# Merging the first transfers of two weights, and halving four sums on GpSimd, in an attention and bilinear-FFN kernel

## The chip, the cores and the metric

The kernel runs on one core of a Trainium2 chip. The metric is the device time of one execution in microseconds (us). A profile is one traced execution; its span is some 1.7 us shorter than the time of the same run (245.2 against 246.89). PE is TensorE, PEld its weight load, DVE is VectorE, ACT is ScalarE, POOL is GpSimd.

A run is labelled slow when it is over 1.5% above the fastest run of the same kernel in the same set. The label compares a kernel only with itself: where all runs of a kernel are equally long, all are labelled fast.

## The reference, cut to what matters

```python
a  = softmax(phi over the sequence)                     # 8 batches, 8 heads, 576 tokens, 32 memories
k_m, v_m = a^T k, a^T v                                 # per head: 32 x 64
x  = softmax(q k_m^T / 8) v_m                           # 4608 tokens x 512
out = ((x @ w_a) * (x @ w_b)) @ w_out                   # 512 -> 1536 -> 512
```

The kernel never forms `x`. It folds `v_m` into the two up weights `w_a` and `w_b` once per batch ("fold"), and multiplies the folded weights (`vab`) by the normalised attention `A`. For the down weight it uses a scheme with fewer products, which needs four sums of quarters of `w_out`; GpSimd makes these once.

## The kernel before

The parts that the argument touches, with cuts marked by `...`:

```python
def load_wab(lo, hi):                     # a column block of both up weights
    nc.gpsimd.dma_start(out=wa_sb[:, :, lo:hi], in_=wa_rows[:, :, lo:hi])
    nc.gpsimd.dma_start(out=wb_sb[:, :, lo:hi], in_=wb_rows[:, :, lo:hi])
...
load_wab(0, 256)
...
load_wab(256, 512)
load_wab(512, 1024)
load_wab(1024, 1536)
load_wo(0)                                # then phi, k, q, v of batch 1, and load_wo(1), load_wo(2)
...
def normalise(g, ...):                    # A = E * R, both in SBUF
    ...
    engine = nc.vector if b < 3 else nc.gpsimd
    engine.tensor_tensor(out=attn[b][:, g, sl], in0=t["E"][:, g, sl], in1=t["R", g][:, sl], op=ALU.mult)
...
def sum_weights():                        # four sums of quarters of the down weight
    t = [w_sums[:, x] for x in range(4)]
    for out, in0, in1 in ((t[0], quarter(0, 1), quarter(0, 0)), (t[1], quarter(1, 1), t[0]),
                          (t[2], quarter(1, 1), quarter(0, 1)), (t[3], quarter(1, 0), t[1])):
        nc.gpsimd.tensor_tensor(out=out, in0=in0, in1=in1, op=ALU.subtract)
...
fill(16)                                  # idle matmuls that wake TensorE's clock
chain(0, "... nr10 nr11 hv0a hx0a")
ups(steps(0, 0, 4), slots(0, "hv0b+hx0b hv1a+hx1a - hv1b+hx1b - v1a+x1a - v1b+x1b"))
load(2)
ups(steps(0, 4, 12), slots(0, "- - - - v2a+x2a+v2b+x2b - -"))
chain(1, "exp0 exp1 y9 ks0 ... vt0 y1 vt1 nr1 hv0a hx0a hv0b y3 hx0b y2")
load(3)                                   # phi, k, v, q of batch 3, issued by GpSimd
sum_weights()                             # and directly behind q's issue, the sums
```

The strings are a plan: `v0a` is the fold of 512 columns (block 0) of `w_a`, `x0a` moves it from PSUM into `vab`; `hv0a` and `hx0a` do so for 256 columns; `nr1` is `normalise` for the second half of the heads; `f2` is two idle matmuls; `y9` nine matmuls of earlier output. In the profiles `pva` is the output of a fold, and `pa` and `pb` are the two up products of one tile of tokens (a "group" is one of them, four matmuls).

The softmax here doesn't subtract the row's maximum and nothing guards it: scores larger than these inputs give would overflow.

Of the kernel before, what the change touches and what calls it, by code (L numbers as in the profile page):

```python
# [11 lines left out]
ALU = mybir.AluOpType  # L12
# [6 lines left out]
def kernel(  # L19
# [11 lines left out]
    nc = tc.nc  # L31
# [60 lines left out]
    def load(b):  # L92
        load_phi(b)
        load_k(b)
        load_v(b)
        load_q(b)

    def load_wab(lo, hi):
        nc.gpsimd.dma_start(out=wa_sb[:, :, lo:hi], in_=wa_rows[:, :, lo:hi])
        nc.gpsimd.dma_start(out=wb_sb[:, :, lo:hi], in_=wb_rows[:, :, lo:hi])  # L100
# [46 lines left out]
    def fill(n, cols=512):  # L147

        pw = banks.tile([P, 512], F32, name="pw")
        for _ in range(n):  # L150
            nc.tensor.matmul(pw[:, :cols], warm[:, :P], warm[:, :cols], start=True, stop=True)
# [2 lines left out]
    make_identity(nc, ident)  # L154
    nc.vector.memset(kv_sbs[0][:, 2], 1.0 / CS)
    nc.vector.tensor_copy(out=kvs[0][:, 0, 0:2], in_=k_f32)
    load_wab(0, 256)

    ones = consts.tile([P, 4, 32], F16, name="ones")
    nc.vector.memset(ones, 1.0)  # L160
# [1 line left out]
                            pattern=[[-32, 4], [0, 32]], channel_multiplier=1)  # L162
    nc.gpsimd.affine_select(out=ones, in_=ones, compare_op=ALU.is_ge, fill=0.0, base=31,
                            pattern=[[32, 4], [0, 32]], channel_multiplier=-1)
    load_wab(256, 512)
    load_wab(512, 1024)
    load_wab(1024, 1536)
    load_wo(0)
# [249 lines left out]
    KH = NFF // 2  # L418
# [3 lines left out]
    def quarter(x, y):  # L422
        return wo_sb[:, KH * x:KH * (x + 1), NH * y:NH * (y + 1)]

    def sum_weights():
        t = [w_sums[:, x] for x in range(4)]
        for out, in0, in1 in ((t[0], quarter(0, 1), quarter(0, 0)), (t[1], quarter(1, 1), t[0]),
                              (t[2], quarter(1, 1), quarter(0, 1)), (t[3], quarter(1, 0), t[1])):
            nc.gpsimd.tensor_tensor(out=out, in0=in0, in1=in1, op=ALU.subtract)

    def tokens_of(cidx, x):
        pair, c = divmod(cidx, NI)
# [151 lines left out]
    def up(b, i, hfs):  # L584
        A, vab = attn[b], vabs[b]
        base = S * (b % 2)
        fs = slice(P * i, P * (i + 1))
        a_sbs = []
        for hf in hfs:
            pa = banks.tile([P, HALF], F32, name="pa")  # L590
            for g in range(2):
                nc.tensor.matmul(pa, vab[0][:, g, fs], A[:, g, HALF * hf:HALF * (hf + 1)],  # L592
                                 start=(g == 0), stop=(g == 1))
            a_sb = apool.tile([P, HALF], F16, name="a_sb")
            nc.scalar.copy(out=a_sb, in_=pa)  # L595
            a_sbs.append(a_sb)
        if len(hfs) > 1:
            yield
        for hf in hfs:
            pb = banks.tile([P, HALF], F32, name="pb")  # L600
            for g in range(2):
                nc.tensor.matmul(pb, vab[1][:, g, fs], A[:, g, HALF * hf:HALF * (hf + 1)],  # L602
                                 start=(g == 0), stop=(g == 1))
            t0 = base + HALF * hf
            nc.vector.tensor_tensor(out=ht[:, i, t0:t0 + HALF], in0=a_sbs[hf - hfs[0]], in1=pb, op=ALU.mult)  # L605
        yield

    def ups(steps, side=()):

        side = iter(side)  # L610
        for step in steps:
            for _ in up(*step):
                work.advance()
                next(side, us[step[0]]["-"])()
        for f in side:
            work.advance()
            f()

    def steps(b, lo, hi):

        return [(b, i, (0, 1)) for i in range(lo, hi)]
# [14 lines left out]
    def slots(b, names):  # L636

        def both(fs):
            return lambda: [f() for f in fs]
        def unit(n):  # L640
            if n == "fin":
                return lambda: work.pull(-work.done % NFF)
            if n == "L":
                return lambda: load(b + 2) if b + 2 < B else None
            if n[0] == "y":
                return lambda: some(int(n[1:]))
            if n[0] == "d" and n[1:].isdigit():
                return lambda: work.pull(int(n[1:]))
            return us[b + n.endswith("'") - n.endswith("_")][n.rstrip("'_")]

        return [both([unit(n) for n in x.split("+")]) for x in names.split()]
# [3 lines left out]
    def some(n):  # L655
        for _ in range(n):
            next(early, None)

    def chain(b, plan):


        for x in plan.split():
            if x[0] == "f":
                fill(int(x[1:]), 256)
            elif x[0] == "y":
                some(int(x[1:]))
            else:
                us[b][x]()

    fill(16)  # L670
    chain(0, "exp0 exp1 ks0 kt0 qt0 qt1 f2 s0 e0 ks1 kt1 den0 qt2 qt3 f2 s1 nr0 e1 vs0 vs1 den1 vt0 vt1 nr10 nr11 hv0a hx0a")
    ups(steps(0, 0, 4), slots(0, "hv0b+hx0b hv1a+hx1a - hv1b+hx1b - v1a+x1a - v1b+x1b"))
    load(2)
    ups(steps(0, 4, 12), slots(0, "- - - - v2a+x2a+v2b+x2b - -"))
    chain(1, "exp0 exp1 y9 ks0 y3 kt0 qt0 qt1 y1 y3 ks1 qt2 s0 e0 y6 kt1 qt3 den0 y3 s1 nr0 e1 y4 y2 den1 vs0 vs1 vt0 y1 vt1 nr1 hv0a hx0a hv0b y3 hx0b y2")
    load(3)
    sum_weights()
    ups(steps(1, 0, 4), slots(1, "- hv1a+hx1a hv1b+hx1b+y1 - v1a+x1a y3+v1b x1b y3"))
    ups(half_steps(1, 0, 4), slots(1, "- v2a+x2a+v2b+x2b+qt0' - - qt1'+exp0'+qt2' exp1' - kv'+km'+y9"))
# [43 lines left out]
```

## Time and profile before

The median is 247.02 us (246.88 to 247.04, 3 runs).

| | before |
|---|---|
| span of the profiled run | 245.2 us |
| TensorE busy | 232.1 us, 95% |
| VectorE, ScalarE, GpSimd busy | 69%, 65%, 63% |
| last weight block used by TensorE | 30.31 us, after a wait of 1.15 us |
| GpSimd's four sums of the down weight | 49.31 to 61.71 us |

TensorE is the bound of the whole, but until 30.3 us the transfers are; the prediction shows the lines.

```profile
48.09 0.45 DVE L325 TENSOR_TENSOR A<-E,R 128x576 f16<-128x576 f16 x1
```

Look at the 0.40 us in which GpSimd idles between the issue of v and the issue of q. VectorE starts its product `A`, two inputs from SBUF, at 48.09, 0.06 us before the issue of v ends (47.41 + 0.74 = 48.15), and does most of it in this gap. Nothing in the program orders the product and the issue of q. Below, the issue of v is called v3 and that of q is called q3, as they are for batch 3.

### The profile page before, as it was taken

What the parts mean: (1) busy time and instruction counts of PE and PEld (TensorE: products, weight loads), DVE (VectorE), ACT (ScalarE), POOL (GpSimd) and SP (SyncE); (2) the same over time, 40 slices, a digit from 0 to 9 for tenths busy, and PEclk for the clock granted to TensorE, in tenths of its full rate; (3) what the DMA queues carried; (4) which work ended last, traced back from release to release, by engine and by line L of the source; (5) the groups of instructions that cost most, each with busy time, mean ns of one, the idle gap of its engine ahead of it and who ended that gap; (6) DMA issues with size and microseconds to landing.
All of it is one profiled execution on the core that took longest, in us unless ns stands there. A gap on an engine that the chain in (4) does not pass through costs nothing.

```text
span 245.2 us, 7629 instructions
## 1 busy us (share of the span) xinstructions
PE 232.1 (95%) x3016; PEld 165.1 (67%) x3016; DVE 168.9 (69%) x406; ACT 158.2 (65%) x409; POOL 154.0 (63%) x126
## 2 busy tenths in 40 slices
PE   7689799999998999999999999999999999999993
PEld 3334474456665857777787777877787877888882
DVE  3455783468959958876995549866996576756742
ACT  2364672678697489578856858577856867565330
POOL 8733263499799028892899769892849177937001
PEclk9977999999999999999999999999999999999999
DMA  6999999999979803973059832598130303032254
GB/s 202 208 198 207 206 257 207 256 218 283 225 190 207 166 1 104 239 133 88 20 138 220 189 86 44 148 189 184 23 68 3 86 3 87 4 87 53 45 128 118
DMA packets 26099, 33.81 MB, mean 138 GB/s; under 512 B 1968, under 2 KB 20528, under 8 KB 26064
## 3 DMA queue, kind: packets, MB, share of 16 engines
q0 software_dynamic: 19344, 22.84, 51.0%
q1 hardware_dynamic: 6208, 9.70, 16.0%
q10 hardware_dynamic: 512, 0.79, 1.0%
q8 instruction: 23, 0.38, 0.6%
q14 instruction: 12, 0.10, 0.1%
HBM read 42.47 MB, written 9.44 MB: 212 GB/s over the span
## 4 chain that ended last, share of the span: by engine, by line
PE 82%; DMA 11%; DVE 3%; issue 1%; ACT 1%; POOL 1%; DVEq 0%; POOLq 0%
PE pa L592 19%; PE pb L602 18%; PE py L462 17%; PE pv L462 8%; DMA wb_sb<-in_moe_w_b_dram 7%; PE pva L337 5%; PE po L389 5%; DMA kv_sb<-in_v_dram 4%; PE px L462 4%; PE pkv L213 2%; PE pD L314 2%; PE pscore L292 1%; PE pT L242 1%; PE pk L256 1%; POOL q_sb L90 1%
## 5 line engine op out<-in xcount | busy, mean ns | idle before, releaser
L605 DVE TENSOR_TENSOR ht<-a_sb,pb 128x288 f16<-128x288 f16 x192 | 83.0, 449 | 41.8 <-ACT a_sb L595 29.2
L595 ACT CAST a_sb<-pa 128x288 f16<-128x288 f32 x192 | 74.9, 406 | 31.0 <-PE pa L592 29.0
L592 PE MATMUL pa<-A,vab 128*128 128x288 f16 x384 | 76.8, 288 | 1.5 <-DVE A L325 1.1
L602 PE MATMUL pb<-A,vab 128*128 128x288 f16 x384 | 77.3, 289 | 0.8 <-ACT vab L349 0.6
L444 POOL TENSOR_TENSOR h_sums<-ht 128x768 f16<-128x768 f16 x28 | 45.9, 1641 | 38.7 <-DVE ht L605 37.3
L602 PEld LDWEIGHTS <-vab 128*128 128x128 f16 x384 | 37.4, 99 | 13.7 <-issue 1.7
L592 PEld LDWEIGHTS <-vab 128*128 128x128 f16 x384 | 34.6, 98 | 15.7 <-issue 8.5
L462 PEld LDWEIGHTS <-h_sums 128*128 128x128 f16 x384 | 37.4, 98 | 6.9 <-issue 0.4
L349 ACT CAST vab<-pva 128x512 f16<-128x512 f32 (+1 forms) x52 | 28.1, 559 | 13.1 <-PE pva L337 13.1
L349 DVE CAST vab<-pva 128x512 f16<-128x512 f32 (+1 forms) x52 | 32.7, 644 | 3.1 <-PE pva L337 2.5
L462 PEld LDWEIGHTS <-ht 128*128 128x128 f16 x288 | 28.2, 98 | 5.6 <-issue 0.4
L462 PE MATMUL py<-w_sums,h_sums 128*128 128x256 f16 x192 | 30.3, 272 | 0.0
L444 POOL TENSOR_TENSOR h_sums<-h_sums,ht 128x768 f16<-128x768 f16 x14 | 23.1, 1648 | 1.0
L444 POOL TENSOR_TENSOR h_sums<-ht,h_sums 128x768 f16<-128x768 f16 x14 | 23.0, 1642 | 1.0
L305 ACT ACTIVATE E<-pscore 128x288 f16<-128x288 f32 x32 | 11.4, 416 | 11.3 <-PE pscore L292 11.2
L325 POOL TENSOR_TENSOR A<-E,R 128x576 f16<-128x576 f16 x10 | 12.8, 1276 | 7.0 <-ACT R L323 6.8
L462 PE MATMUL py<-wo_sb,ht 128*128 128x256 f16 x96 | 16.0, 273 | 0.0
L462 PE MATMUL pv<-w_sums,h_sums 128*128 128x256 f16 x96 | 16.0, 272 | 0.0
L469 ACT ACTIVATE u<-py 128x256 f32<-128x256 f32 x32 | 12.4, 388 | 5.2 <-PE py L462 4.9
L462 PE MATMUL py<-w_sums,ht 128*128 128x256 f16 x96 | 15.5, 272 | 0.1
L462 PE MATMUL px<-wo_sb,ht 128*128 128x256 f16 x96 | 15.4, 273 | 0.0
L204 DVE STREAM_TRANSPOSE qT<-q_sb 128x288 f32<-128x288 f32 x32 | 14.3, 462 | 0.6 <-DMA q_sb<-in_q_dram 0.6
(64 smaller groups left out, 262.9 us busy)
## 6 DMA issues: line engine op xcount, KB each, us to landing
out_dram<-o_sb SPq DMA_DIRECT2D x68, 128.0 KB, 2.5
kv_sb<-in_v_dram POOLq DMA_DIRECT2D x7, 576.0 KB, 11.1
phi_sb<-in_phi_dram POOLq DMA_DIRECT2D x7, 576.0 KB, 4.8
kv_sb<-in_k_dram POOLq DMA_DIRECT2D x7, 576.0 KB, 8.6
q_sb<-in_q_dram POOLq DMA_DIRECT2D x6, 576.0 KB, 14.0
wo_sb<-in_moe_w_out_dram POOLq DMA_DIRECT2D x3, 512.0 KB, 16.3
q_sb<-in_q_dram POOLq DMA_DIRECT2D x4, 288.0 KB, 12.5
wa_sb<-in_moe_w_a_dram POOLq DMA_DIRECT2D x2, 512.0 KB, 14.9
```

The source lines that it names most:

```text
L204: nc.vector.transpose(out=t["qT"][:, hp, :].bitcast(F32), in_=qs[b][:, hp, :].bitcast(F32))
L325: engine.tensor_tensor(out=attn[b][:, g, sl], in0=t["E"][:, g, sl], in1=t["R", g][:, sl], op=ALU.mult)
L337: nc.tensor.matmul(t["pva", lo, z][g][0][32 * j:32 * j + 32, 0:hi - lo], t["kvT"][64 * r:64 * r + 64, 4 + g, M * j:M * j + M], w_sbs[z][64 ...
L349: engine_copy(out=vabs[b][z][:, g, lo:hi], in_=pva[:, 0:hi - lo])
L389: nc.tensor.matmul(po, ht[:, i, P * c:P * (c + 1)], wo_sb[:, i, :], start=(i == 0), stop=(i == NFF - 1))
L444: engine.tensor_tensor(out=out, in0=in0, in1=in1, op=op)
L462: nc.tensor.matmul(po, lhs[:, i], rhs[:, i], start=first and i == 0, stop=i == KH - 1, skip_group_check=not first)
L469: nc.scalar.mul(out=x, in_=po, mul=scale)
L592: nc.tensor.matmul(pa, vab[0][:, g, fs], A[:, g, HALF * hf:HALF * (hf + 1)], start=(g == 0), stop=(g == 1))
L595: nc.scalar.copy(out=a_sb, in_=pa)
L602: nc.tensor.matmul(pb, vab[1][:, g, fs], A[:, g, HALF * hf:HALF * (hf + 1)], start=(g == 0), stop=(g == 1))
L605: nc.vector.tensor_tensor(out=ht[:, i, t0:t0 + HALF], in0=a_sbs[hf - hfs[0]], in1=pb, op=ALU.mult)
```

## The change

Its intent: fewer, larger transfers for the first block of the up weights, the folds of which then come in one piece; and shorter GpSimd instructions, so that VectorE is held off for less time by each.

```diff
-    load_wab(0, 256)
+    load_wab(0, 512)
...
-    load_wab(256, 512)
     load_wab(512, 1024)
...
-            nc.gpsimd.tensor_tensor(out=out, in0=in0, in1=in1, op=ALU.subtract)
+            for x in range(2):
+                sl = slice(KH // 2 * x, KH // 2 * (x + 1))
+                nc.gpsimd.tensor_tensor(out=out[:, sl], in0=in0[:, sl], in1=in1[:, sl], op=ALU.subtract)
...
-    chain(0, "... nr10 nr11 hv0a hx0a")
-    ups(steps(0, 0, 4), slots(0, "hv0b+hx0b hv1a+hx1a - hv1b+hx1b - v1a+x1a - v1b+x1b"))
+    chain(0, "... nr10 nr11 v0a x0a")
+    ups(steps(0, 0, 4), slots(0, "v0b+x0b - - - - v1a+x1a - v1b+x1b"))
```

More of the change, by code (lines that the diff above doesn't have):

```diff
@@ L670 @@
     fill(16)
-    chain(0, "exp0 exp1 ks0 kt0 qt0 qt1 f2 s0 e0 ks1 kt1 den0 qt2 qt3 f2 s1 nr0 e1 vs0 vs1 den1 vt0 vt1 nr10 nr11 hv0a hx0a")
-    ups(steps(0, 0, 4), slots(0, "hv0b+hx0b hv1a+hx1a - hv1b+hx1b - v1a+x1a - v1b+x1b"))
+    chain(0, "exp0 exp1 ks0 kt0 qt0 qt1 f2 s0 e0 ks1 kt1 den0 qt2 qt3 f2 s1 nr0 e1 vs0 vs1 den1 vt0 vt1 nr10 nr11 v0a x0a")
+    ups(steps(0, 0, 4), slots(0, "v0b+x0b - - - - v1a+x1a - v1b+x1b"))
     load(2)
```

## The prediction

> **What bounds the kernel now.** I read the page first, then the chain that ended last in order of time for the first 40 us, then GpSimd's and TensorE's timelines of that stretch, then tables by stretch cut at the steps of the granted clock. The page gives the frame:
>
> ```profile
> PE 232.1 (95%) x3016; PEld 165.1 (67%) x3016; DVE 168.9 (69%) x406; ACT 158.2 (65%) x409; POOL 154.0 (63%) x126
> ```
>
> TensorE is the bound of the whole, but not of its beginning. The chain in order of time says:
>
> ```profile
> 3.60 10.12 DMA kv_sb<-in_v_dram
> ...
> 14.01 16.26 DMA wb_sb<-in_moe_w_b_dram
> ...
> 30.31 0.41 PE pva L337 x8
> 30.72 0.60 PE pb L602 x4
> ```
>
> Until 30.3 us the end is set by transfers: the last one is the third block (columns 1024 to 1536) of the second up weight. After that the chain is nearly all matmuls. So a change before 30.3 us moves the end only if it moves that landing, or makes TensorE so late that it no longer waits for it. How much room there is stands in TensorE's timeline:
>
> ```profile
> 16.39 0.69 PE L337 MATMUL pva<-wa_sb,kvT 64*32 64x256 f16 x8
> 17.56 0.66 PE L592 MATMUL pa<-A,vab 128*128 128x288 f16 x4 [0.48 <-ACT vab L349]
> 18.16 0.30 PE L337 MATMUL pva<-wb_sb,kvT 64*32 64x256 f16 x8
> 19.05 1.14 PE L602 MATMUL pb<-A,vab 128*128 128x288 f16 x4 [0.59 <-ACT vab L349]
> ...
> 28.75 0.41 PE L337 MATMUL pva<-wa_sb,kvT 64*32 64x512 f16 x8
> 30.31 0.41 PE L337 MATMUL pva<-wb_sb,kvT 64*32 64x512 f16 x8 [1.15 <-DMA wb_sb<-in_moe_w_b_dram]
> ```
>
> The slack is 1.15 us: TensorE could arrive that much later at 30.31 for nothing. GpSimd's timeline shows when weights land, because its 13th issue waits for the 5th to land, the 14th for the 6th and so on (eight in flight):
>
> ```profile
> 16.53 0.74 POOL L104 DMA_DIRECT2D wo_sb<-in_moe_w_out_dram  x1 [1.79 <-DMA wa_sb<-in_moe_w_a_dram]
> 17.71 0.75 POOL L78 DMA_DIRECT2D phi_sb<-in_phi_dram  x1 [0.44 <-DMA wb_sb<-in_moe_w_b_dram]
> 19.03 0.74 POOL L82 DMA_DIRECT2D kv_sb<-in_k_dram  x1 [0.56 <-DMA wa_sb<-in_moe_w_a_dram]
> 20.36 0.70 POOL L90 DMA_DIRECT2D q_sb<-in_q_dram  x1 [0.59 <-DMA wb_sb<-in_moe_w_b_dram]
> ```
>
> The four 256 KB pieces landed just before 16.5, 17.7, 19.0 and 20.4 us. The 512 KB pieces after them came 2.5 to 2.6 us apart (issues at 22.93, 25.50, 28.02, 30.55). Last, the table by stretch (columns: stretch, length, busy of PE, PEld, DVE, ACT, POOL, granted clock, DMA share, GB/s):
>
> ```profile
> 12.08:15.50 3.42, 3.42 (x105) 1.74 (x102) 2.06 (x6) 2.37 (x6) 0.74 (x1) 0.50 1.38 199
> 15.50:18.91 3.41, 1.83 (x28) 0.65 (x24) 1.66 (x6) 2.38 (x8) 1.49 (x2) 1.00 1.42 198
> 18.91:22.32 3.41, 3.27 (x20) 1.60 (x20) 1.44 (x5) 1.25 (x4) 1.44 (x2) 0.50 1.25 207
> 22.32:25.73 3.41, 3.41 (x43) 1.68 (x42) 2.91 (x8) 2.21 (x6) 0.98 (x2) 1.00 1.24 206
> 32.56:245.20 212.64, 206.09 (x2662) 152.15 (x2660) 150.70 (x363) 142.33 (x371) 137.94 (x98) 1.00 0.62 127
> ```
>
> The transfers never pause: about 200 GB/s in every stretch, and 198 against 206 while the small pieces move. The clock falls to half in stretches of 3.41 us that follow a sparse one (1.83 us busy at 15.50 to 18.91). From 32.56 us on TensorE is 97% busy (206.09 / 212.64) at the full clock.
>
> **What the Trainium skill says.** "TensorE: Matmul & The Clock Gate", section "Part 1: The HAM clock gate", has windows of about 3.4 us, half rate after an idle window and full rate after a busy one. The trace agrees in length and in direction; where the limit lies it leaves open (2.27 us busy kept the clock, 2.24 lost it). "DMA: Bandwidth & Descriptors", section "Rules for kernel authors", advises coalescing transfers, and under "Why small descriptors are slow (HBM only)" gives a fixed cost per packet; here it shows only as the 198 against 206 GB/s. "GPSIMD Engine Reference", section "1. Specifications", says that its SBUF interface is shared with VectorE, with contention when a VectorE instruction has two SBUF inputs. The trace agrees elsewhere: a product of A at 73.28 us, both inputs in SBUF, took 1.46 us beside a GpSimd sum, against 0.46 without.
>
> **Part one, the transfers.** Four pieces of 256 KB become two of 512 KB, in the order a, b instead of a, b, a, b. Bytes and queue order behind them stay.
> - Columns 0 to 512 of a land where two pieces did, at about 17.4 us instead of 16.3; those of b where four did, at about 20.0 instead of 17.5.
> - What comes behind them gains the lower packet cost: 1 MB at 206 instead of 198 GB/s, 5.1 instead of 5.3 us, so 0.2 us. The last block lands at about 30.05 instead of 30.27. Two issues fewer let GpSimd queue the next ones earlier, which is worth nothing as the queue is never empty.
>
> **Part two, the folds of the first batch.** Removed: two 256-column folds and their evictions; the remaining two become 512 wide (0.41 instead of 0.30 us at full clock; evictions 0.59 and 0.69 instead of 0.37 and 0.42). Step by step:
> - fold of a at 17.4, evicted by 18.5; pa of tile 0 at 18.6 instead of 17.56.
> - fold of b at 20.0; twice 0.41 if at half clock, then 0.69 of eviction: pb of tile 0 at 21.4 instead of 19.05, 2.35 us late.
> - then no fold stands between pa1, pb1, pa2 and pb2. In the kernel before there are two, 0.41 and 0.30, and their waits.
> At full clock four matmuls of a group take 0.49 us (chain: 0.49 for pa and pb), at half about 0.95 (20.47 to 21.40 in the timeline). The fold of block 1 of a, at 23.94 before, comes after five groups:
> - (i) clock full from 22.32: 21.4 + 0.95 + 4 x 0.49 = 24.3 us. The rest follows as before about 0.35 late, well inside the 1.15 us. TensorE then waits for the last block, and the end moves by -0.2.
> - (ii) clock half until 25.73: by then four and a half groups are done; the fold is at about 26.0, 2.05 late. From there seven groups and two folds remain before block 2: 7 x 0.49 + 2 x 0.41 = 4.25, so 30.25, and with block 2's two folds, 0.82 (0.41 each), pb of tile 6 at 31.05 against 30.65: +0.4. ScalarE and VectorE must evict without a gap in this catch-up, so I count up to +0.7.
> Which one comes is set by the window 18.91 to 22.32. In it TensorE now waits for b's transfer for over a microsecond, so it is busy about 2.2 us instead of 3.27, which is at the undecided limit. I give (ii) 6 in 10.
>
> **Part three, the halves.** Four sums of 3.09 us (49.31 to 61.71) become eight of 128x768, a shape that GpSimd does in 1.64 us in the token sums, starts 1.65 us apart (63.14, 64.86, 66.57, 68.17, 69.75): 8 x 1.65 = 13.2 instead of 12.4, so an end at 62.5. The next GpSimd work starts at 63.14 after an idle 1.43 us, so 0.6 us of room remain. VectorE in this stretch does only products from PSUM, casts from PSUM and transposes, at their usual 446, 688 and 455 ns, so nothing waits for a GpSimd sum that a shorter one would free: 0 us.
>
> **Sum.** 0.4 x (-0.2) + 0.6 x (+0.4) is +0.15 us; the end of (ii) leans upward. 247.02 + 0.1 = 247.1 us.
>
> **Rivals.**
> - The up weights become the bound earlier and TensorE never catches up: late by the full 2.35 us at pb0 less the 1.15 us of slack, +1.2, 248.2 us. For it: the half clock. Against it: two folds fewer and 0.49 us groups with all weights there.
> - The merge is hidden altogether and only the packet cost counts: 246.8 us. For it: the 1.15 us wait at 30.31. It is my case (i).
> - The merge makes all later transfers a good deal earlier: between the landing of v (13.72) and of the first piece (16.3) lie 2.6 us where 1.3 would do, and if the small packets cause that, the last block is 1.3 us earlier, 245.9 us. Against it: the rate in that time is 198 GB/s, so bytes were moving and only their order is odd.
> - The halves let VectorE in between and speed up the stretch from 49 to 62 us: at most some tenths, as VectorE's durations there are normal.
>
> **Range and chances.** Low end: (i) with some of the early landing, 246.4. High end: (ii) with a clumsy catch-up, 248.0. Two per cent are 4.9 us; all rivals lie within 1.3. Faster 0.01, same 0.975, slower 0.015.
>
> **What would show it.** The granted clock in 22.3 to 25.7 us tells (i) from (ii). The fold of a near 17.4 us, pb of tile 0 near 21.4. The wait at the last block's fold: about 1 us in (i), none in (ii). Eight sums of about 1.64 us, ending near 62.5, with an idle gap after them. It would be wrong if the last block landed over 0.5 us off 30.05, if the lead or lag at 32 us did not reach the end, or if the token sums started later than 63.1 by more than TensorE's own lag.

## More of the kernel before

Timeline columns: start, length, engine, line, operation, tiles, count, and in brackets the idle time before it and what ended that.

```profile
47.41 0.74 POOL L85 DMA_DIRECT2D kv_sb<-in_v_dram  x1 [2.24 <-PE pT L274]
48.55 0.74 POOL L90 DMA_DIRECT2D q_sb<-in_q_dram  x1 [0.40 <-DVE A L325]
49.31 3.11 POOL L429 TENSOR_TENSOR w_sums<-wo_sb 128x1536 f16<-128x1536 f16 x1
```

## The result, and the profile after

Four runs of the changed kernel took 246.72, 261.45, 247.32 and 262.68 us. Two are labelled fast and two slow. Four runs of the kernel before, in the same rounds, took 246.88 to 247.10. The ratio of fast runs is 1.0001, with an interval of 0.9976 to 1.0025. Here and below a ratio is the mean time of one kernel's fast runs over that of the other's of the same rounds, so it is not quite the ratio of the medians that are quoted. The median of all four runs, 254.38, is a time that no run had.

The profiled run was a fast one, with a span of 245.0 us. On its page, TensorE's row of busy times is:

```profile
PE 231.8 (95%) x3000; PEld 165.3 (67%) x3000; DVE 168.4 (69%) x404; ACT 157.9 (64%) x407; POOL 153.0 (62%) x128
```

There are 16 matmuls fewer, the two folds of eight that fell away, and two more instructions on GpSimd: two issues fewer, four sums more. TensorE's timeline in the first 31 us:

```profile
17.30 0.63 PE L336 MATMUL pva<-wa_sb,kvT 64*32 64x512 f16 x8 [0.85 <-DMA wa_sb<-in_moe_w_a_dram]
18.62 1.14 PE L593 MATMUL pa<-A,vab 128*128 128x288 f16 x4 [0.70 <-ACT vab L348]
19.77 0.63 PE L336 MATMUL pva<-wb_sb,kvT 64*32 64x512 f16 x8
21.10 1.14 PE L603 MATMUL pb<-A,vab 128*128 128x288 f16 x4 [0.70 <-ACT vab L348]
...
29.86 0.41 PE L336 MATMUL pva<-wa_sb,kvT 64*32 64x512 f16 x8
30.09 0.40 PE L336 MATMUL pva<-wb_sb,kvT 64*32 64x512 f16 x8
30.42 0.66 PE L603 MATMUL pb<-A,vab 128*128 128x288 f16 x4
```

The beginning is 2.05 us later than before (pb of tile 0 at 21.10 against 19.05), but the last fold has no bracket any more: the wait of 1.15 us for the last block is gone, and TensorE leaves this part 0.23 us earlier (30.42 against 30.65). The chain that ended last has only one piece of transfer in this stretch, the first, and matmuls and evictions (moves from PSUM to SBUF) from there on:

```profile
4.92 12.24 DMA wa_sb<-in_moe_w_a_dram
17.30 0.70 PE pva L336 x6
```

GpSimd's timeline shows the last landing by the issue that waits for it, 0.36 us earlier than before (30.55):

```profile
30.19 0.70 POOL L85 DMA_DIRECT2D kv_sb<-in_v_dram  x1 [1.87 <-DMA wb_sb<-in_moe_w_b_dram]
```

The table by stretch (columns as in the prediction) shows the granted clock in the stretches that the prediction was undecided about:

```profile
18.91:22.32 3.41, 2.70 (x18) 1.27 (x17) 1.13 (x2) 1.38 (x3) 0.70 (x1) 0.50 1.24 208
22.32:25.73 3.41, 3.41 (x27) 2.13 (x26) 2.12 (x7) 1.71 (x5) 1.41 (x2) 0.76 1.24 205
```

The clock came back within the second stretch, 0.76 on average: between the prediction's two cases. The trace's clock records have it at half from 17.15 to 23.98 us, two windows of 3.41 us, which do not lie where the stretches, cut by the steps of the kernel before, do. So far everything is small and near the prediction. It does not explain the two runs of 261 and 263 us. The first profile shows nothing of them, since it was a fast run.

### The profile page after: what moved, and what is told of

Its sections match the earlier page's. It is cut to its first block, busy times and chain, and to the rows that moved or that the text cites. A ratio compares the mean times of both kernels' runs of the same rounds, so it can differ in the third digit from the quotient of the medians.

```text
span 245.0 us, 7595 instructions
## 1 busy us (share of the span) xinstructions
PE 231.8 (95%) x3000; PEld 165.3 (67%) x3000; DVE 168.4 (69%) x404; ACT 157.9 (64%) x407; POOL 153.0 (62%) x128
## 4 chain that ended last, share of the span: by engine, by line
PE 86%; DMA 5%; DVE 3%; ACT 2%; POOL 1%; issue 1%; DVEq 0%; POOLq 0%
PE pa L593 21%; PE pb L603 20%; PE py L463 17%; PE pv L463 8%; PE pva L336 6%; DMA wa_sb<-in_moe_w_a_dram 5%; PE po L388 5%; PE px L463 4%; PE pkv L212 2%; PE pD L313 2%; PE pscore L291 1%; PE pT L241 1%; ACT vab L348 1%; PE pk L255 1%; POOL q_sb L90 1%
## 5 line engine op out<-in xcount | busy, mean ns | idle before, releaser
L470 ACT ACTIVATE u<-py 128x256 f32<-128x256 f32 x32 | 12.4, 388 | 5.2 <-PE py L463 4.9
```

Source lines behind the costliest of these rows:

```text
L470: nc.scalar.mul(out=x, in_=po, mul=scale)
```

## The experiments

The theory at the outset: the long runs are of the kernel's own making, something in the stretch of GpSimd's sums that happens or not by a small difference in timing. The rival: they are a slower state of the chip, which any kernel may meet, and the clock of 0.95 in them is its cause. A second question was which of the two parts of the change is at fault. All kernels gave correct results. Kernels of one set ran on the same chip beside the kernel before.

### First set (kernel before: 247.03 to 247.47 us, 11 runs)

**The changed kernel again** (no edit), for a trace of a long run.

> The changed kernel once more, with more runs, because two of its first four came out at 261.5 and 262.7 us at a mean granted clock of 0.954 and 0.957, against 246.7 and 247.3 us at 0.986 and 0.972; the kernel before had four runs within 0.2 us. Theory S (the slow runs are the change's own: its sparser beginning meets the clock windows at an unlucky moment): about half of the runs are slow again, the kernel before beside it on the same chip has none. Rival C (a state of the chip or of its neighbours that hits any kernel): no slow run, or as many in the kernel before. The fast runs by both: 246.5 to 247.4 us, ratio 0.998 to 1.002.

Measured: 261.97, 262.39, 262.83 and 261.72 us; ratio 1.0606 (1.0593 to 1.0620). All are long here, so they are labelled fast. The kernel before ran at 247.0 to 247.5 between them on the same chip, so a slower state of the chip falls as the cause. The trace has the cause in one line of VectorE's timeline:

```profile
48.92 13.90 DVE L324 TENSOR_TENSOR A<-E,R 128x576 f16<-128x576 f16 x1
```

The product that took 0.45 us took 13.90. GpSimd's timeline beside it:

```profile
48.25 0.74 POOL L85 DMA_DIRECT2D kv_sb<-in_v_dram  x1 [2.98 <-PE pT L273]
48.98 0.75 POOL L90 DMA_DIRECT2D q_sb<-in_q_dram  x1
49.73 3.25 POOL L430 TENSOR_TENSOR w_sums<-wo_sb 128x768 f16<-128x768 f16 x2
...
59.29 3.21 POOL L430 TENSOR_TENSOR w_sums<-wo_sb,w_sums 128x768 f16<-128x768 f16 x2
```

There is no bracket at q3: GpSimd went from v3 to q3 without a gap, and through all eight sums. The product ended at 62.82, 0.32 us after the last sum (59.29 + 3.21 = 62.50). Meanwhile TensorE waited for what VectorE was to do after the product. The table of waits (engine, tile and line, what it waited for: us in total, times, longest), and the table by stretch:

```profile
PE pa L593 <- DVE vab L348: 12.4, 1, 12.4
```

```profile
18.91:22.32 3.41, 2.33 (x16) 1.08 (x16) 0.78 (x2) 1.38 (x3) 0.70 (x1) 0.51 1.24 208
22.32:25.73 3.41, 3.41 (x16) 2.06 (x14) 1.73 (x4) 1.41 (x4) 0.99 (x2) 0.50 1.24 205
55.00:60.00 5.00, 0.00 (x0) 0.00 (x0) 5.00 (x1) 0.00 (x0) 5.00 (x4) 0.50 1.14 289
```

At 55 to 60 us TensorE did nothing, VectorE counted as busy with a single instruction, and the clock was lost as a consequence. The sum: 12.4 us of wait and 2.3 us more of busy time at the lower clock (234.1 against 231.8) make 14.7 of the 15.3 us between the spans of 260.3 and 245.0. The first two rows show something else, taken up below: here the clock stayed at half through both (the trace's clock records have it at half from 18.98 to 25.81 us). And when it was back, TensorE's weight load for `pb` waited for ScalarE's eviction of the fold just before:

```profile
28.66 0.10 PEld L603 LDWEIGHTS <-vab 128*128 128x128 f16 x1 [0.41 <-ACT vab L348]
```

**The merged transfers and wide folds alone** (the changed kernel with the sums whole again):

```diff
-            for x in range(2):
-                sl = slice(KH // 2 * x, KH // 2 * (x + 1))
-                nc.gpsimd.tensor_tensor(out=out[:, sl], in0=in0[:, sl], in1=in1[:, sl], op=ALU.subtract)
+            nc.gpsimd.tensor_tensor(out=out, in0=in0, in1=in1, op=ALU.subtract)
```

> The merged transfers with the 512-wide folds, the GpSimd sums whole as before. My theory: the halves are worth nothing, so the fast runs equal the changed kernel's, 246.5 to 247.3 us, and theory S expects slow runs here as often as in the changed kernel. Rival H (the halves matter, for the time or for the slow runs): the fast runs differ from the changed kernel's by over 0.5 us, or there is no slow run here.

Measured: three runs at 247.02 to 247.28 (ratio of fast runs 0.9997, 0.9983 to 1.0011) and three labelled slow at 252.09 to 252.50. There are two kinds of run without the halves too, but the long ones are 5 us longer, not 15. That is between the two expectations: there are slow runs, and the halves do matter for their length. The traced run was a short one, so it only shows the gap of 0.23 us and a product of 0.45.

**The halves alone** (the kernel before with the loop over halves):

```diff
-            nc.gpsimd.tensor_tensor(out=out, in0=in0, in1=in1, op=ALU.subtract)
+            for x in range(2):
+                sl = slice(KH // 2 * x, KH // 2 * (x + 1))
+                nc.gpsimd.tensor_tensor(out=out[:, sl], in0=in0[:, sl], in1=in1[:, sl], op=ALU.subtract)
```

> The kernel before with the GpSimd sums in halves and nothing else. My theory: eight sums of 1.6 us end near 62.5 us, the token sums still start at 63.1, so 246.9 to 247.1 us, ratio 1.000, and no slow run. Rival H: a gain or a loss of over 0.5 us, or slow runs at 261 us here.

Measured: 247.15 to 247.82 us; ratio 1.0009 (0.9996 to 1.0022), no long run. The halves by themselves cost nothing that these runs show, though four runs can't exclude a rare long one. Neither part alone gave 262.

**The merged transfers with the folds of 256 columns kept** (the kernel before with):

```diff
-    load_wab(0, 256)
+    load_wab(0, 512)
...
-    load_wab(256, 512)
```

> The transfers merged, the folds left at 256 columns as before. It tells the later landing from the wider fold. My theory: the fold of the first weight starts near 17.3 us and the first fold of the second near 19.8, as in the changed kernel, the evictions are 0.3 us shorter and two more folds stand in the way; TensorE reaches the last block within 0.5 us of the changed kernel, so 246.6 to 247.4 us. If the wider folds alone were what saves time, this one is slower than the kernel before by the 2 us of later landing less the 1.15 us of wait, about 247.9. Slow runs: theory S expects them here too, as its beginning is as sparse.

Measured: 250.32, 251.09, 250.32 and 250.58 us; ratio 1.0135 (1.0122 to 1.0148), above everything that was expected. This is the first trace of a long run with whole sums: no gap at q3, the product took 4.24 us (48.62 to 52.86), TensorE waited 2.8 us. The first whole sum ended at 52.53, so the product ended 0.33 us after the first sum and not after all four.

What these traces have in common led to the theory for the next two sets: **if q3's issue follows v3's without a gap, the product is shut out until the train of GpSimd's sums has its first gap.** A whole sum that needs the sum directly before it leaves one: 49.43 + 3.10 = 52.53, and the second whole sum starts at 52.62. Among the halves none needs the one directly before it: where one needs another at all, that one is two or more places back. So there is no gap. And the gap at q3 is there if TensorE is early: v3's issue is released by TensorE's own progress, q3's by the landing of the third block of the down weight, the eighth transfer before it.

### Second set (kernel before: 246.46 to 247.32 us, 11 runs)

**The kernel before, with TensorE made late**, by nine idle matmuls in the chain of batch 1. Transfers, folds and sums are as before.

```diff
-    chain(1, "exp0 exp1 y9 ks0 ...")
+    chain(1, "exp0 exp1 f9 y9 ks0 ...")
```

> The kernel before with nine idle matmuls of 256 columns (about 0.11 us each, 1.0 us) put in front of batch 1's sums, so that TensorE is a microsecond later against the stream of transfers, whatever the clock did. Theory P: in the slow runs VectorE's second product of A (two operands in SBUF) finds GpSimd still in the issue of v for batch 3 and then in one instruction after another, because the issue of q no longer has to wait for the third block of the down weight to land (near 48.1 us); it is shut out until the sums leave a gap. So this kernel is slow in every run: 1.0 for the matmuls and 3 to 5 us for a product shut out for about one whole sum (4.2 us in the run with merged transfers alone), 250.5 to 253 us. Rival K (the slow runs are the half clock of the beginning itself, or a state of the chip): 248.0 to 248.4 us, no more than the matmuls cost.

Measured: 250.96 to 252.88 us, median 252.42; ratio 1.0208 (1.0180 to 1.0236). GpSimd's and VectorE's timelines:

```profile
48.86 0.74 POOL L85 DMA_DIRECT2D kv_sb<-in_v_dram  x1 [3.22 <-PE pT L274]
49.59 0.75 POOL L90 DMA_DIRECT2D q_sb<-in_q_dram  x1
50.35 3.10 POOL L429 TENSOR_TENSOR w_sums<-wo_sb 128x1536 f16<-128x1536 f16 x1
53.54 3.18 POOL L429 TENSOR_TENSOR w_sums<-wo_sb,w_sums 128x1536 f16<-128x1536 f16 x1
```

```profile
49.54 4.24 DVE L325 TENSOR_TENSOR A<-E,R 128x576 f16<-128x576 f16 x1
```

Lateness alone, with nothing of the change, makes the 4.24 us product. The gap that lets it in is seen in the start of the second sum, 53.54, 0.09 us after the first one's end (50.35 + 3.10 = 53.45).

**The same lateness with the halves** (both edits above).

> The same nine matmuls, with the GpSimd sums in halves, all transfers and folds as before. Theory P: the sums in halves leave no gap, as no half waits for the one just before it, so the product is shut out for all eight of them, some 13 to 14 us: 260.5 to 263.5 us in every run. Rival K: 248.0 to 248.5 us. If the length of one GpSimd instruction set the wait, halves would wait less than whole sums: under 250.

Measured: 262.72 to 263.35 us; ratio 1.0659 (1.0645 to 1.0674). The product took 13.90 us, TensorE's wait was 12.4, as in the changed kernel's long runs, without any of the merged transfers. So the long runs are lateness times halves: lateness with whole sums 252, halves without lateness 247, both 263.

**The changed kernel with a guard**: GpSimd copies one column of `A` between v3 and q3, so q3 can't be issued before the product is done.

```diff
-    load(3)
+    load_phi(3)
+    load_k(3)
+    load_v(3)
+    nc.gpsimd.tensor_copy(out=guard, in_=attn[1][:, 1, 0:1])
+    load_q(3)
```

> The changed kernel with one GpSimd copy of one column of that product of A between the issues of v and q for batch 3, so that GpSimd stands still until VectorE has done it. Theory P: no run near 262; every run 246.6 to 248.3 us, the late ones up to 1 us over the others. Rival K: runs at 262 us as often as before.

Measured: 247.61 to 247.94 us, median 247.89; ratio 1.0039 (1.0027 to 1.0051). TensorE was late (v3 at 48.43, later than in the long run above), and the product took 0.45 us. So lateness without the shutting out, the guard's own wait included, costs 0.9 us, and the rest of the 15 us is the shutting out.

**The changed kernel with TensorE kept warm**: 26 idle matmuls of 256 columns at the places where it waits for the first two blocks.

```diff
-... nr10 nr11 v0a x0a")
-    ups(steps(0, 0, 4), slots(0, "v0b+x0b - - ..."))
+... nr10 nr11 f10 v0a f5 x0a")
+    ups(steps(0, 0, 4), slots(0, "f5+v0b+f6+x0b - - ..."))
```

> The changed kernel with idle matmuls of 256 columns in the waits of the beginning (10 before the fold of a, 5 behind it, 5 before and 6 behind the fold of b), so that the stretch after 15 us is not sparse and the clock stays full. Theory P with the clock: TensorE reaches the last block of the up weights before it lands at about 29.9 us, waits for it and so is in step with the transfers again; 246.6 to 247.3 us in every run, none at 262. If the clock has no part in it: the runs split as in the changed kernel, or all are slow as TensorE is kept up by the extra matmuls.

Measured: 246.02 to 247.05 us in six runs, median 246.49; ratio 0.9985 (0.9971 to 0.9999), no long run; three of them lie below the expected 246.6. The table by stretch and TensorE's timeline:

```profile
20.00:25.00 5.00, 5.00 (x58) 3.22 (x50) 3.81 (x9) 2.97 (x8) 1.35 (x3) 1.00 1.24 207
```

```profile
29.67 0.41 PE L336 MATMUL pva<-wb_sb,kvT 64*32 64x512 f16 x8 [0.91 <-DMA wb_sb<-in_moe_w_b_dram]
```

At the full clock TensorE catches up and waits 0.91 us for the last block, as the kernel before did, and the gap at q3 was 0.62 us. The changed kernel itself wasn't run on this chip, but the guard's run shows its beginning late there: a clock at half until 26.89 us, and pb of tile 6 at 31.68 against 30.02 here. So the clock is the link between the merged transfers and the lateness.

### Third set (kernel before: 246.96 to 247.33 us in ten runs, and one of 252.55)

The one long run of the kernel before, labelled slow, is of the size that the whole sums give. It has no trace. It is one in 37 runs of that kernel.

**The kernel before with its gap filled** by a small idle sum on GpSimd between v3 and q3, to see whether any instruction directly behind v3 shuts the product out.

```diff
-    load(3)
+    load_phi(3)
+    load_k(3)
+    load_v(3)
+    nc.gpsimd.tensor_tensor(out=idle, in0=warm[:, :256], in1=warm[:, 256:], op=ALU.add)
+    load_q(3)
```

> The kernel before, TensorE not late, with one idle GpSimd sum (128x256 of zeros, about 0.6 us) between the issues of v and q for batch 3, that is, in the gap of 0.3 to 0.4 us in which VectorE's product of A got in. Theory P: it is the gap that lets the product in, so here it is shut out until the first whole sum ends: every run slow, 250 to 252.5 us. Rival L (lateness itself makes the runs slow, not the gap): 246.9 to 247.4 us, as 0.6 us of GpSimd have room before its next wait.

Measured: 246.47 to 247.27 us; ratio 0.9997 (0.9984 to 1.0011). The expectation missed. It is the time that rival L, lateness itself, had named; against L stands the guard's run, late and yet at 247.9. GpSimd's and VectorE's timelines:

```profile
47.82 0.74 POOL L86 DMA_DIRECT2D kv_sb<-in_v_dram  x1 [2.25 <-PE pk L257]
48.57 0.89 POOL L680 TENSOR_TENSOR idle<-warm 128x256 f16<-128x256 f16 x1
49.43 0.77 POOL L91 DMA_DIRECT2D q_sb<-in_q_dram  x1
```

```profile
48.50 0.45 DVE L326 TENSOR_TENSOR A<-E,R 128x576 f16<-128x576 f16 x1
```

There was no gap behind v3, and the product ran at its usual 0.45 us; it had started 0.07 us ahead of the idle sum, just as it starts 0.06 ahead of q3 in the long runs. So the theory's wording "no gap behind v3" is too wide. A sum directly behind v3 does not shut the product out; a transfer's issue there did in all four traces that have it (0 us of gap, in the table below). Why the two differ, no run here tells. The idle sum took 0.89 us; a straight line through the sums of 768 and 1536 columns (1.64 and 3.10) gives 0.67 for its 256, an estimate, so it may be the sum that waited for the product here.

**Lateness with the halves in another order**: first all four sums of one half, then of the other, so that the second sum needs the one directly before it, and leaves a gap.

```diff
-            for x in range(2): ...             # inside the loop over the four sums
+        for x in range(2):                     # outside of it, and f9 in chain 1 as above
+            for out, in0, in1 in (...):
```

> The nine late matmuls and the sums in halves, but in the order of all four sums for the first half and then all four for the second, so that most halves wait for the one just before them, as the whole sums do. Theory P: GpSimd stands still for about 0.1 us at such a wait and the product gets in behind the first half, some 2.5 us after it came instead of 13.9: 249 to 251 us. Rival: it is the number of GpSimd instructions in a row, then 262 to 263.5 us as with the halves side by side.

Measured: 247.24, 249.59, 247.12 and 249.60 us; ratio 1.0054 (1.0014 to 1.0093). It is half a miss: two runs are short. The traced one of them was not late enough (gap of 0.23 us, product 0.45); the other has no trace. The other two, at 249.6, are 13.6 us below the 263.2 of the same lateness with the change's order. That fits a train whose first gap comes after 1.7 us (in the trace the first half ends at 49.48 + 1.66 = 51.14 and the second starts at 51.23), but those two runs have no trace, so it is not shown.

**The kernel before with the last fold two slots later**, to be rid of the 1.15 us wait at 30.31 us.

```diff
-slots(0, "- - - - v2a+x2a+v2b+x2b - -"))
+slots(0, "- - - - v2a+x2a - v2b+x2b"))
```

> The kernel before with the last fold of the second up weight moved from behind pa of tile 6 to behind pa of tile 7, as tile 8 is the first that needs it. TensorE then does two groups (1.0 us) in the wait of 1.15 us for the last block. If all that follows is bound by TensorE: 245.9 to 246.3 us. If the transfers for batch 1 bind next: no gain, 246.9.

Measured: 246.16 to 247.63 us, median 246.93; ratio 0.9992 (0.9977 to 1.0006). Over six runs this is the second of the two expectations, no gain. In the trace the wait is gone, and the traced run, the shortest of the six, fits the first; over all six nothing is left of that gain. Where it is given back in the longer runs, no trace shows.

**All of it together**: the warm kernel with the guard, the later fold, and the halves in the other order.

> The merged transfers with the idle matmuls in the waits, the later fold, the GpSimd copy that waits for the product of A, and the halves in the chained order. From the warm kernel's 246.5 us less about 0.9 us of its wait for the last block: 245.5 to 246.1 us, no slow run.

Measured: 246.26 to 247.38 us, median 246.66; ratio 0.9989 (0.9976 to 1.0001). A miss too, and no better than the warm kernel, which remains the best with 0.15% less time than the kernel before (and has no guard: its order still hangs on the timing).

## Why the prediction was right, and what it did not see

The forecast of no change held for the runs that came out short, and that two of the four did is in part luck: on the chip of the first set all four were 6% longer.

The table gives, for the traced run of each kernel without a guard or filling, the start of v3, the landing of the third block of the down weight as the trace records it, the idle time before q3, and the length of the product.

| kernel | v3 starts | landing | gap before q3 | product |
|---|---|---|---|---|
| before | 47.41 | 48.02 | 0.40 | 0.45 |
| changed, short run | 47.18 | 47.61 | 0.23 | 0.45 |
| merged only, short run | 47.47 | 47.90 | 0.23 | 0.45 |
| halves only | 47.82 | 48.31 | 0.29 | 0.45 |
| reordered halves, late (short run) | 47.76 | 48.20 | 0.23 | 0.45 |
| changed, warm | 46.77 | 47.60 | 0.62 | 0.45 |
| before, fold later | 46.13 | 47.59 | 1.25 | 0.45 |
| changed, long run | 48.25 | 47.97 | 0 | 13.90 |
| merged transfers, narrow folds | 47.94 | 47.89 | 0 | 4.24 |
| before, late | 48.86 | 48.39 | 0 | 4.24 |
| halves, late | 48.82 | 48.34 | 0 | 13.90 |

The columns separate without an exception: where the landing came 0.43 us or more after v3's start there was a gap and the product ran, and where it came before v3's start there was none and the product was shut out. The profile's brackets put the end of the gap down to VectorE, but q3 starts 0.53 or 0.54 us after the landing in all seven traces with a gap, so it is the landing that releases it. The product's own arrival doesn't differ: in every trace, short or long, it starts 0.67 or 0.68 us after v3. What differs is only what GpSimd does next.

v3 follows TensorE: from before to the changed kernel's short run, its long run and the warm kernel, pb of tile 6 moved by -0.23, +0.84 and -0.63 us (30.65 before; 30.42, 31.49, 30.02), and v3 moved by -0.23, +0.84 and -0.64. So where TensorE stands at 30 us is where it stands at 48, when that is decided. And where it stands at 30 us follows the clock: in the four traces with merged transfers, wide folds and no idle matmuls the half clock ended at 23.98 (changed, short), 24.57 (merged only), 25.81 (changed, long) and 26.89 us (guard), and pb of tile 6 came at 30.42, 30.71, 31.49 and 31.68. In four of the six traces that begin and fold as the kernel before does, a wait of 1.15 to 1.45 us for the last block puts TensorE back in step with the transfers. In the other two (halves late, and filled) the half clock ended at 23.73 and 24.11 us, against 22.32 in the profile before, and there is no such wait, so the kernel before is not held in step in every run, which fits its one long run. In the four traces just named the wait is gone: the change left the step to the clock.

Now by the prediction's own steps:

- **Part one, the transfers, held in direction.** The fold of a began at 17.30 (predicted 17.4), the last block landed in time for an issue at 30.19, 0.36 us earlier than before (predicted 0.22). But this is one pair of traces. Over all traces the same issue lies at 29.84 to 31.03 with the old transfers (seven, mean 30.61) and at 29.81 to 30.60 with the merged ones (seven, mean 30.23), so the size is not resolved.
- **Part two, the folds, had the right mechanism, but not what decides between its cases.** In the short run pb of tile 0 came at 21.10 (21.4), and 0.23 us were gained at tile 6 (0.2 in case (i)), which reached the end: the span went from 245.2 to 245.0. That this agrees is partly luck: the fold of block 1 of a, at 25.05, lies between case (i), 24.3, and case (ii), 26.0, and the wait for the last block that was to mark case (i) is missing. The long run is case (ii): half clock until 25.81, the fold at 26.12 (26.0). What told the two apart was not what the prediction named, whether one window or two are at half: both runs had two, the long one's 1.83 us later. The window "busy about 2.2" was not "at the undecided limit" either. That limit was read at the full clock; from the half clock, in all traces up to 75 us, the 16 windows with up to 2.85 us of TensorE busy (as the profile counts it) were followed by another at half, and the 14 with 2.88 or more by one at full. The first window at half had 2.40 us in the short run and 2.33 in the long one.
- **The size of case (ii) was off too.** "4.25" for seven groups and two folds measured 4.81 (26.12 to 30.93), the last two folds 0.56 instead of 0.82, and "+0.4", leaning up to +0.7, became +0.84. The term that was too small is the catch-up, and not for its clock, which was full: the two groups behind the fold of b took 0.77 and 0.71 us (starts 27.89, 28.66, 29.37) instead of 0.49, with the wait for an eviction that is shown above; the prediction had allowed for this only in its lean to +0.7. In the run with the guard (+1.03 at tile 6) a third window was at half.
- **Part three, the halves, failed, in the words "so nothing waits for a GpSimd sum that a shorter one would free: 0 us".** The sums themselves were as told: eight from 48.90 to 61.72, followed by an idle 1.19 us. What failed was the stretch that was searched. It began with the first sum, at 49.31; the one VectorE instruction with two SBUF inputs ended at 48.54, 0.77 us before it, and only a gap of 0.40 us kept it there. In long runs it fell into the sums, and it did not wait for one sum but for the whole train.
- **The number** 247.1 holds for the short runs (246.72 and 247.32). The range, up to 248.0, holds none of the long runs: not the two of the result, nor the four of the first set. All rivals were thought to lie within 1.3 us; the one that mattered, 15 us, was not among them. The rival that said that shorter sums would let VectorE in had the effect upside down: it was the wait between two whole sums that let it in, and the halves took this away.

What stays open is why a transfer's issue shuts the product out where a sum in the same place doesn't, and how often each chip falls to each side: the changed kernel was long in two of four runs, and then in four of four on the chip of the first set.

## What to carry to other kernels

When a change removes a wait that most runs share, ask what that wait kept in step; what came before another engine's work by a few tenths of a microsecond may now come after it. List the instructions that two engines can shut each other out of, also those that end just before the stretch, and give such an order a dependence (here a copy of one column) rather than luck. Look at every run's time: a kernel with two kinds of run has no median worth quoting, and where the other kernel, run in between on the same chip, stays short, a long run is not the chip's state.

## What the Trainium skill lacked or had wrong

- "SBUF — State Buffer", section "Who interferes with whom", says that a VectorE instruction with two SBUF inputs contends with a GpSimd instruction that reads SBUF, and, of VectorE's two-port modes, that whoever issues first holds the shared pair "for the whole instruction". The contention is here, but a product was shut out for a train of instructions: 13.90 us through eight sums of some 1.6 us, ending 0.32 us after the last. With whole sums it got in at the first gap of 0.09 us, after 4.24 us. The section has nothing on trains, nor on a dependence between two instructions making the gap.
- The same section says "Issue order, not op shape, decides who blocks", and infers that such a product doesn't hold off the making of descriptors; of the opposite direction it says nothing. Here the outcome went with the kind of GpSimd's next instruction: with a transfer's issue 0.05 or 0.06 us behind the product's start it was shut out (four traces, 4.24 or 13.90 us), with a sum 0.07 us behind it was not (one trace, 0.45 us). No page has this.
- "TensorE: Matmul & The Clock Gate", section "Part 1: The HAM clock gate", takes the warm-up as under 1% of a kernel. The direct cost of the lateness here agrees (0.9 us of 247, in the run with the guard), but the phase of the windows also decided on which side of a 0.2 us gap GpSimd fell: the short and the long run of the changed kernel both had two windows at half, 1.83 us apart, and took 247 and 262 us. Nor does a page say how busy a window must be: here 2.88 us of 3.41 ended the half clock and 2.85 did not, while from the full clock windows of 1.80 to 2.24 us went either way (all traces, up to 75 us).
